# Scores between a slot's two groups of transposes, the exponential between their evictions, and a third bank for some of the transposes

## The chip, the cores and the metric

One core of a Trainium2 chip runs the whole program. TensorE (PE, with its weight loads as PEld), VectorE (DVE), ScalarE (ACT), GpSimd (POOL) and the DMA queue that SyncE (SP) issues work side by side; each takes its own instructions strictly in order, and semaphores hold an instruction back until what it reads is there and what it overwrites has been read. The metric is the time of one execution in microseconds (us), as a median of several runs.

## The reference

Three parts follow each other:

```python
q_assign = np.argmax(einsum(q_n, c_n)); k_assign = np.argmax(einsum(k_n, c_n))   # 16 clusters per head
mask = q_assign[:, :, :, None] == k_assign[:, :, None, :]
scores = np.where(mask, scale * q @ k.T, -1e9)
attn = softmax(scores); x = attn @ v                      # batch 2, 8 heads, 768 rows, head size 64
x = softplus(x @ w_in1) @ w_out1                          # 1536 tokens, 512 -> 2048 -> 512
x = (h * clip(h + 3, 0, 6) / 6) @ w_out2, h = x @ w_in2
```

Attention is confined to rows of the same cluster, and two feed-forward layers follow. The weights come as 64-bit floats.

## The kernel before, in words

Products are made of fp32r operands split into a high and a low part. The heads are worked in 8 pairs (batch by two heads); a pair has 12 slots, one for each head and block of 128 query rows, so there are 96 slots, numbered through from 0 or, where a pair is meant, from 0 to 11. A main loop runs over the slots. In slot s:

- `scores(s + 3)`: four matmuls of Q and K into a PSUM tile `s` (two of them), where two extra groups of rows carry the cluster mask; `row_max` on DVE makes `nm`, the negated row maximum; `expo` on ACT makes `pr`, the exponentials, and their row sums in `sums`.
- `flip(s, 0)` and `flip(s, 1)`: two groups of three transposes of `pr` into a PSUM bank `t`; ACT evicts a group to `pth` (high part), and DVE then makes `ptl` (low part) from `t` and `pth`. The bank is free when `ptl` is done. Pool `ps_t` has two banks, which the groups take in turn.
- `weigh`: four matmuls of `vs` (the values) with `pth` and `ptl` of three slots earlier into `pv`; after every third slot `gather` lets ACT copy `pv` to the tiles `xs`.

Around these stand `extras(s, place)`: a table written by hand (`at(slot, place, function, ...)`) that puts the rest at one of seven places of a slot, with `o` the first slot of the pair before the one that is being prepared. For the next pair: `p_sims` (cluster similarities, `psm`), `p_sims_out` (`sT`), `p_back` (transposed back, `pbk`), `p_max`, `p_equal`, `p_rank`, `p_best`, `p_first` (the first best cluster, as a one-hot matrix), `p_onehot` (transposed, `po`), `p_mask` (`mk`), and `assemble`, `assemble_mask`, which copy the pieces to Q and K by DMA. For the pair before: `total` (`rs`), `tot_flip` (`pb`), `tot_out` (`rT`), `tot_spread` (the DMAs `row` and `rsb`), `fin_*`. All PSUM tiles of this work use one bank, tag `prep` of pool `ps_p`, one after another. Weight pieces are fetched and converted at table places too (`convert_*`), and the first matmuls of the first layer (`phase_a`, tile `h`) are put into slots 88 to 96. The order within each engine is the order in which the code is written.

After the loop the two layers run; PE works through 96 steps of 12 plus 12 matmuls.

Of the kernel before, what the change touches and what calls it, by code (L numbers as in the profile page):

```python
# [8 lines left out]
F32 = mybir.dt.float32  # L9
# [13 lines left out]
def cluster_attention_then_two_mlps(  # L23
# [149 lines left out]
    def attention():  # L173
        with ExitStack() as st, ExitStack() as st_ld, ExitStack() as st_ps:
# [4 lines left out]
            pp = pool("pp", 2)  # L179
# [36 lines left out]
            cent = cb.tile([P, NPAIR * (C + D)], F32, name="cent")  # L216
            cT = cent[:, :NPAIR * C].rearrange("p (n c) -> p n c", c=C)
# [114 lines left out]
            def p_equal(n):  # L332
                d = prep[n]
                sv, mx = d["pb"], d["mx"]
                eq = sm.tile(full, F32, tag="eq", name="eq", bufs=1)
                nc.vector.tensor_tensor(eq, sv, mx.unsqueeze(2).to_broadcast(full), ALU.is_equal)
                d["eq"] = eq
# [12 lines left out]
            def p_first(n):  # L350
                d = prep[n]
                oh = sm.tile(full, BF16, tag="oh", name="oh", bufs=1)
                nc.vector.tensor_tensor(oh, d["eq"], d["mx2"].unsqueeze(2).to_broadcast(full), ALU.is_equal)
# [74 lines left out]

            def flip(t, g):
# [5 lines left out]
                pt = ps_t.tile([P, 512], F32, tag="t", name="t")  # L435
# [22 lines left out]
            def gather(h, step):  # L458
# [6 lines left out]
                if step == 0:  # L465
# [20 lines left out]
            def tot_out(n):  # L486
                rT = sm.tile([2 * NJ, P], F32, tag="rT", name="rT", bufs=1)
# [41 lines left out]
            for n in range(NP):  # L529
                o = SL * n - SL  # L530
                if n > 1:
# [19 lines left out]
                    at(o + 2, 2, p_equal, n)  # L551
                    at(o + 2, 4, p_rank, n)
                    at(o + 4, 2, p_best, n)
                    at(o + 5, 2, p_first, n)
                    at(o + 6, 3, p_onehot, n)
                    at(o + 7, 1, p_mask, n)
                    at(o + 4, 1, assemble, n, 0)
                    at(o + 7, 2, assemble_mask, n, 0)
# [26 lines left out]
                if n < NP - 1:  # L585
                    at(o + -2, 4, total, n)
                    at(o + 3, 0, tot_flip, n)
                    at(o + 3, 4, tot_out, n)
# [107 lines left out]
            c_sq = sm.tile([P, HALF], F32, tag="eq", name="c_sq", bufs=1)[:, :NPAIR * D].rearrange("p (n d) -> p n d", d=D)  # L696
# [24 lines left out]

            p_centroids(0)
# [30 lines left out]
            oh = sm.tile(full, BF16, tag="oh", name="oh", bufs=1)  # L753
            nc.vector.memset(oh, 0.0)
# [62 lines left out]
            for s in range(-3, NS + 7):  # L817
                extras(s, 0)
                if 2 <= s + 1 < NS:
                    expo(s + 1)  # L820
                extras(s, 1)
                if 2 <= s + 2 < NS:
                    row_max(s + 2)
                extras(s, 2)
                if 0 <= s < NS:
                    flip(s, 0)
# [4 lines left out]
                if 2 <= s + 3 < NS:  # L831
                    scores(s + 3)
                extras(s, 5)
                h, c = s // JH - 1, s % JH
                if 0 <= h < 4 * NP:
                    weigh(h, c)
                    if c == JH - 1:
                        for step, where in enumerate((2, 2, 4)):
# [180 lines left out]
```

## Time and profile before

| | |
|---|---|
| median of 3 runs | 782.77 us (782.29 to 786.18) |
| the profiled execution | 782.03 us |
| its span, first to last instruction | 780.2 us |
| TensorE busy in the span | 768.9 us |
| DVE, ACT, POOL busy in the span | 456.3, 416.9, 151.0 us |
| granted TensorE clock, mean | 0.999 |

The time is the whole execution; the span lies within it, and rows give times from the span's start. The attention part takes roughly the first 250 us, the layers the rest. A busy engine is not one at its peak: rows of PE overlap each other, so gaps between starts say more than busy time.

### The profile page before, as it was taken

The numbers are of one execution on the slowest core, as the hardware profiler recorded it, in microseconds if no ns is written. First come the engines' busy times: TensorE is split into PE (matmuls) and PEld (weight loads), VectorE is DVE, ScalarE is ACT, GpSimd is POOL, SyncE is SP. The second block draws the span as 40 slices with busy tenths as digits, with TensorE's granted clock in tenths as the row PEclk, the third lists the DMA queues.
The fourth block names the chain that finished last, engine by engine and source line by source line (L and its number), as shares of the span: only waits on it lengthen the run. The fifth ranks groups of instructions, "written<-read, shape, count | busy, mean of one in ns | idle before, by whom it ended". The sixth has DMA issues, their size and how long they took to land.

```text
span 780.2 us, 10575 instructions
## 1 busy us (share of the span) xinstructions
PE 768.9 (99%) x3841; PEld 642.1 (82%) x3841; DVE 456.3 (58%) x788; ACT 416.9 (53%) x830; POOL 151.0 (19%) x222
## 2 busy tenths in 40 slices
PE   7999999999999999999999999999999999999998
PEld 6788888888888788888888888888888888888886
DVE  6988888888988999721111276879752322232222
ACT  6899988988998766522122254545532222222221
POOL 3666756856434000000000000000000000000000
PEclk9999999999999999999999999999999999999999
DMA  7647667557381760000000365640000100010001
GB/s 190 186 128 178 145 158 188 136 157 172 87 249 56 267 240 0 1 1 0 1 1 27 110 207 176 210 135 0 1 1 0 55 1 0 1 55 0 1 1 54
DMA packets 39124, 69.75 MB, mean 89 GB/s; under 512 B 4480, under 2 KB 24096, under 8 KB 39072
## 3 DMA queue, kind: packets, MB, share of 16 engines
q1 hardware_dynamic: 39072, 69.08, 30.9%
q8 instruction: 30, 0.49, 0.3%
q14 instruction: 22, 0.18, 0.1%
HBM read 46.30 MB, written 3.19 MB: 63 GB/s over the span
## 4 chain that ended last, share of the span: by engine, by line
PE 88%; DVE 5%; ACT 3%; issue 1%; POOL 1%; DMA 1%; POOLq 0%; ACTq 0%; DVEq 0%; SPq 0%
PE h L169 32%; PE y L895 17%; PE y L893 16%; PE t L438 7%; PE s L408 6%; PE pv L453 6%; PE psm L308 2%; DVE ptl L443 1%; DVE nm L416 1%; ACT pth L442 1%; ACT pr L424 1%; DMA rsb<-row 0%; DMA row<-rT 0%; PE warm L245 0%; ACT xs L468 0%
## 5 line engine op out<-in xcount | busy, mean ns | idle before, releaser
L169 PE MATMUL h<-xhi,pi 128*128 128x512 f32 x768 | 238.5, 392 | 0.6 <-DVE pi L144 0.5
L169 PEld LDWEIGHTS h<-xhi,pi 128*128 128x128 f32 x768 | 143.8, 188 | 32.3 <-DVE pi L144 1.0
L874 DVE TENSOR_TENSOR glo<-g,ghi 128x512 fp32r<-128x512 f32 x96 | 66.3, 691 | 146.2 <-ACT ghi L861 117.4
L169 PE MATMUL h<-xlo,pi 128*128 128x512 f32 x384 | 149.9, 390 | 0.0
L895 PE MATMUL y<-po,ghi 128*128 128x512 f32 x384 | 118.9, 391 | 0.0
L893 PE MATMUL y<-ghi,po 128*128 128x512 f32 x384 | 118.8, 391 | 0.0
L443 DVE TENSOR_TENSOR ptl<-t,pth 128x384 fp32r<-128x384 f32 x192 | 97.8, 550 | 28.0 <-ACT pth L442 27.8
L867 DVE SCALAR_TENSOR_TENSOR g<-u,h 128x512 f32<-128x512 f32 x48 | 33.0, 688 | 127.2 <-ACT u L863 127.1
L863 ACT ACTIVATE u<-h,half 128x512 f32<-128x512 f32 x48 | 33.0, 687 | 128.3 <-PE h L169 128.0
L416 DVE TENSOR_REDUCE nm<-s 128x1 f32<-128x768 f32 x96 | 90.7, 945 | 3.7 <-PE s L408 3.7
L442 ACT ACTIVATE pth<-t 128x384 fp32r<-128x384 f32 x192 | 85.7, 487 | 11.8 <-PE t L438 11.4
L408 PE MATMUL s<-K,Q 128*128 128x256 f32 (+1 forms) x384 | 89.9, 356 | 1.7 <-ACT pr L424 1.1
L438 PE MATMUL t<-ident,pr 128*128 128x128 f32 x576 | 88.3, 280 | 1.2 <-DVE ptl L443 0.7
L424 ACT ACTIVATE pr<-s,nm 128x768 f32<-128x768 f32 x96 | 86.5, 901 | 3.5 <-DVE nm L416 3.2
L860 ACT ACTIVATE g<-h 128x512 f32<-128x512 f32 x48 | 28.5, 595 | 110.8 <-PE h L169 110.8
L169 PEld LDWEIGHTS h<-xlo,pi 128*128 128x128 f32 x384 | 72.1, 188 | 15.7
L895 PEld LDWEIGHTS y<-po,ghi 128*128 128x128 f32 x384 | 72.1, 188 | 15.6
L893 PEld LDWEIGHTS y<-ghi,po 128*128 128x128 f32 x384 | 72.0, 188 | 15.6
L438 PEld LDWEIGHTS t<-ident,pr 128*128 128x128 f32 x576 | 64.0, 140 | 20.4 <-DVE ptl L443 15.4
L408 PEld LDWEIGHTS s<-K,Q 128*128 128x128 f32 x384 | 65.8, 189 | 11.5 <-ACT pr L424 2.3
L895 PE MATMUL y<-po,glo 128*128 128x512 f32 x192 | 75.1, 391 | 0.0
L893 PE MATMUL y<-glo,po 128*128 128x512 f32 x192 | 75.0, 391 | 0.0
(123 smaller groups left out, 937.9 us busy)
## 6 DMA issues: line engine op xcount, KB each, us to landing
ri<-in_moe_w_in SPq DMA_DIRECT2D x29, 512.0 KB, 4.6
ro<-in_moe_w_out SPq DMA_DIRECT2D x29, 512.0 KB, 4.8
K<-hik SPq DMA_DIRECT2D x31, 192.0 KB, 5.3
Q<-hiq SPq DMA_DIRECT2D x15, 384.0 KB, 4.1
Q<-loq SPq DMA_DIRECT2D x16, 192.0 KB, 5.6
v<-in_v SPq DMA_DIRECT2D x8, 384.0 KB, 6.6
rsb<-row SPq DMA_DIRECT2D x16, 192.0 KB, 3.8
out<-o SPq DMA_DIRECT2D x12, 256.0 KB, 3.5
```

The costliest lines, as they stand in the source:

```text
L169: nc.tensor.matmul(hs[n][:, :TB], w[:, c, :], x[c][:, cols], start=(c == 0 and i == 0), stop=(c == NC - 1 and i == 2))
L408: nc.tensor.matmul(ps[:, n0:n1], Q[i][:, u, j * P:(j + 1) * P], K[i][:, u, n0:n1], start=(u == 0), stop=(u == 1),)
L416: nc.vector.tensor_reduce(nm, st_s[t][:, :S], AX.X, ALU.max, negate=True)
L424: nc.scalar.activation(pr, st_s.pop(t)[:, :S], AF.Exp, bias=st_p[t], accum_out=sums_of[n][:, i, j:j + 1])
L438: nc.tensor.transpose(pt[:, c * P:(c + 1) * P], pr[:, kt * P:(kt + 1) * P], ident)
L442: last_flip[:] = [nc.scalar.activation(dh, src, AF.Copy)]
L443: nc.vector.tensor_tensor(dl, src, f32(dh), ALU.subtract)
L453: nc.tensor.matmul(st_v[h][:, :HALF], vs[:, kt, i, :], st_t[h][u][:, kt, :], start=(kt == 0 and u == 0), stop=(kt == NJ - 1 and u == 1),)
L863: nc.scalar.activation(t["u"], t["h"], AF.Relu, bias=half, scale=1.0 / 6.0)
L874: nc.vector.tensor_tensor(t["glo"], t["g"], f32(t["ghi"]), ALU.subtract)
L893: nc.tensor.matmul(y[:, :TB], w[:, e, :], x, **fl)
L895: nc.tensor.matmul(y, x[:, e * P:(e + 1) * P], w.rearrange("p c e -> p (c e)"), **fl)
```

## The change

In a slot, the order of the loop changes. Before: exponential of s + 1, row_max of s + 2, both groups of transposes, scores of s + 3, weigh. Now: group 0, exponential of s + 2, scores of s + 3 and their row_max, group 1, weigh. `pr` gets a third buffer for that. In slots 4, 5, 8, 9 and 10 of pairs 1 to 6 every third group goes to the `prep` bank instead of a bank of `ps_t`: those are group 0 of slots 4 and 10 and group 1 of slots 5 and 8 (also slots 8 and 10 of pair 0). The gather of a pair's first head is one activation of all 128 partitions, with a DMA for the half that belongs to the other tile, and gathers now stand at place 0 of their slot. `p_equal`, `p_best`, `p_first`, `p_onehot`, `p_mask`, `tot_flip` and `tot_out` move to later or other places. `eq` is bf16 and holds the one-hot matrix too; `cent` borrows a load buffer, and its part `cT` is copied by POOL at the start; `oh`, `rT` and `c_sq` share buffers with other tiles.

```diff
-            pp = pool("pp", 2)
+            pp = pool("pp", 3)
...
-            cent = cb.tile([P, NPAIR * (C + D)], F32, name="cent")
-            cT = cent[:, :NPAIR * C].rearrange("p (n c) -> p n c", c=C)
+            cent = ld.tile([P, S], F32, tag="v", name="cent")[:, :NPAIR * (C + D)]
+            cT = cb.tile([P, NPAIR, C], F32, name="cT")
...
-                eq = sm.tile(full, F32, tag="eq", name="eq", bufs=1)
+                eq = sm.tile(full, BF16, tag="eq", name="eq", bufs=1)
...
-                oh = sm.tile(full, BF16, tag="oh", name="oh", bufs=1)
-                nc.vector.tensor_tensor(oh, d["eq"], d["mx2"].unsqueeze(2).to_broadcast(full), ALU.is_equal)
+                oh = d["eq"]
+                nc.vector.tensor_tensor(oh, oh, d["mx2"].unsqueeze(2).to_broadcast(full), ALU.is_equal)
...
+            def third_bank(t, g):
+                return 8 <= t < NS - SL and t % SL in (4, 5, 8, 9, 10) and (2 * t + g) % 3 == 2
+
             def flip(t, g):
...
-                pt = ps_t.tile([P, 512], F32, tag="t", name="t")
+
+                pl, tag = (ps_p, "prep") if third_bank(t, g) else (ps_t, "t")
+                pt = pl.tile([P, 512], F32, tag=tag, name="t")
...
-                if step == 0:
+                if i == 0:
+
+                    if step == 0:
+                        nc.scalar.activation(main, pv[:, :HALF], AF.Copy)
+                        nc.sync.dma_start(rest[a:a + D], main[z:z + D])
+                elif step == 0:
...
-                rT = sm.tile([2 * NJ, P], F32, tag="rT", name="rT", bufs=1)
+                rT = sm.tile([2 * NJ, P], F32, tag="sT", name="rT", bufs=1)
...
-                    at(o + 2, 2, p_equal, n)
+                    at(o + 2, 4, p_equal, n)
                     at(o + 2, 4, p_rank, n)
-                    at(o + 4, 2, p_best, n)
-                    at(o + 5, 2, p_first, n)
-                    at(o + 6, 3, p_onehot, n)
-                    at(o + 7, 1, p_mask, n)
+                    at(o + 4, 4, p_best, n)
+                    at(o + 5, 4, p_first, n)
+                    at(o + 6, 4, p_onehot, n)
+                    at(o + 6, 6, p_mask, n)
...
-                    at(o + 7, 2, assemble_mask, n, 0)
+                    at(o + 7, 1, assemble_mask, n, 0)
...
-                    at(o + 3, 0, tot_flip, n)
-                    at(o + 3, 4, tot_out, n)
+                    at(o + 3, 4, tot_flip, n)
+                    at(o + 3, 6, tot_out, n)
...
+            nc.gpsimd.tensor_copy(cT.rearrange("p n c -> p (n c)"), cent[:, :NPAIR * C])
             p_centroids(0)
...
-            oh = sm.tile(full, BF16, tag="oh", name="oh", bufs=1)
-            nc.vector.memset(oh, 0.0)
+            oh = sm.tile(full, BF16, tag="sT", name="oh", bufs=1)
+            nc.gpsimd.memset(oh, 0.0)
...
-                if 2 <= s + 1 < NS:
-                    expo(s + 1)
+                if 0 <= s < NS:
+                    flip(s, 0)
                 extras(s, 1)
                 if 2 <= s + 2 < NS:
-                    row_max(s + 2)
+                    expo(s + 2)
                 extras(s, 2)
-                if 0 <= s < NS:
-                    flip(s, 0)
+                if 2 <= s + 3 < NS:
+                    scores(s + 3)
+                    row_max(s + 3)
                 extras(s, 3)
                 if 0 <= s < NS:
                     flip(s, 1)
                 extras(s, 4)
-                if 2 <= s + 3 < NS:
-                    scores(s + 3)
                 extras(s, 5)
...
-                        for step, where in enumerate((2, 2, 4)):
+                        for step, where in enumerate((0, 0, 4)):
```

What this moves on the engines stands in the order of the built programs. First PE, slot 3 of a steady pair and the head of slot 4; `[waits ...]` names the engines whose semaphore holds a row back. Before:

```order
L483 MATMUL pb<-ident,rs 12x128 [waits DVE_49]
L438 MATMUL t<-ident,pr 128x128 [waits DVE_49]
L438 MATMUL t<-ident,pr 128x128 x2
L438 MATMUL t<-ident,pr 128x128 [waits DVE_49]
L438 MATMUL t<-ident,pr 128x128 x2
L408 MATMUL s<-K_156,Q_154 128x512 [waits DMAHW5_49,DMAHW4_49,DMAHW6_49,DMAHW3_49,Activation_49]
L408 MATMUL s<-K_156,Q_154 128x512 [waits DMAHW2_49,DMAHW7_49,DMAHW1_49,DMAHW0_49]
L408 MATMUL s<-K_156,Q_154 128x256 x2
L453 MATMUL pv<-pth,vs 128x384 [waits PE_49,Activation_49]
```

The same slot now, up to the first transposes of slot 4:

```order
L443 MATMUL t<-ident,pr 128x128 [waits DVE_49]
L443 MATMUL t<-ident,pr 128x128 x2
L408 MATMUL s<-K_157,Q_155 128x512 [waits DMAHW5_49,DMAHW4_49,DMAHW6_49,DMAHW3_49,Activation_49]
L408 MATMUL s<-K_157,Q_155 128x512 [waits DMAHW2_49,DMAHW7_49,DMAHW1_49,DMAHW0_49]
L408 MATMUL s<-K_157,Q_155 128x256 x2
L443 MATMUL t<-ident,pr 128x128 [waits DVE_49]
L443 MATMUL t<-ident,pr 128x128 x2
L493 MATMUL pb<-ident,rs 12x128 [waits DVE_49]
L458 MATMUL pv<-pth,vs 128x384 [waits PE_49,Activation_49]
L458 MATMUL pv<-ptl,vs 128x384
L458 MATMUL pv<-pth,vs 128x384
L458 MATMUL pv<-ptl,vs 128x384
L443 MATMUL t<-ident,pr 128x128 [waits Activation_49]
```

The scores now part the two groups of transposes, `pb` went behind them, and the group at the head of slot 4 waits for ACT where the others wait for DVE: it uses the bank that `pb` had.

Second, ACT in the same slot: the gathers (`xs`), the evictions (`pth`), the exponential (`pr`) and `rT`, which empties `pb`. Before:

```order
L424 ACTIVATE pr,sums<-s,nm 128x768 [waits DVE_49,Activation_49]
L466 ACTIVATE xs_1970<-pv 64x384 [waits PE_49]
L468 ACTIVATE xs_1969<-pv 64x384
L442 ACTIVATE pth<-t 128x3x128 [waits PE_49] x2
L488 ACTIVATE rT<-pb 12x128 [waits DMAHW3_49]
L424 ACTIVATE pr,sums<-s,nm 128x768 [waits DVE_49,Activation_49]
```

And now:

```order
L447 ACTIVATE pth<-t 128x3x128 [waits PE_49]
L476 ACTIVATE xs_1968<-pv 64x384 [waits PE_49]
L478 ACTIVATE xs_1967<-pv 64x384 [waits DMAHW0_49]
L447 ACTIVATE pth<-t 128x3x128 [waits PE_49,Activation_49]
L424 ACTIVATE pr,sums<-s,nm 128x768 [waits DVE_49,Activation_49]
L447 ACTIVATE pth<-t 128x3x128 [waits PE_49]
L498 ACTIVATE rT<-pb 12x128 [waits PE_49,Activation_49]
L447 ACTIVATE pth<-t 128x3x128 [waits PE_49]
```

The exponential moved from ahead of the gathers to between the evictions, so it stands between the gathers and `rT`.

Third, DVE in slots 4 and 5 of such a pair, where `p_best` (`mx<-eq`) and `p_first` (to `oh`, now to `eq`) stand. Before:

```order
L416 TENSOR_REDUCE nm<-s 128x1 [waits PE_49]
L348 TENSOR_REDUCE mx_1804<-eq 128x24 [waits Pool_49]
L443 TENSOR_TENSOR ptl<-t,pth 128x3x128 [waits Activation_49] x2
L416 TENSOR_REDUCE nm<-s 128x1 [waits DVE_49,PE_49]
L353 TENSOR_TENSOR oh<-eq,mx_1804 128x384 [waits DVE_49]
L443 TENSOR_TENSOR ptl<-t,pth 128x3x128 [waits Activation_49] x2
```

And now:

```order
L416 TENSOR_REDUCE nm<-s 128x1 [waits PE_49]
L448 TENSOR_TENSOR ptl<-t,pth 128x3x128 [waits Activation_49]
L348 TENSOR_REDUCE mx_1827<-eq 128x24 [waits Pool_49]
L448 TENSOR_TENSOR ptl<-t,pth 128x3x128 [waits Activation_49]
L416 TENSOR_REDUCE nm<-s 128x1 [waits DVE_49,PE_49]
L448 TENSOR_TENSOR ptl<-t,pth 128x3x128 [waits Activation_49]
L353 TENSOR_TENSOR eq<-eq,mx_1827 128x384 [waits DVE_49]
```

Both steps moved from ahead of the slot's `ptl` to behind its second one.

## Rows read from the trace of the kernel before

**Rows 1.** Stretches: span, busy us of PE, PEld, DVE, ACT, POOL, clock, DMA.
```profile
20.00:40.00 20.00, 18.74 (x115) 14.47 (x114) 18.90 (x32) 17.37 (x39) 12.89 (x19) 1.00 0.67 182
140.00:160.00 20.00, 19.99 (x129) 16.85 (x129) 17.93 (x31) 19.02 (x45) 17.16 (x24) 1.00 0.60 145
```

**Rows 2.** Timeline of PE: start us, length us, line, operation, tiles, shape, count.
```profile
26.19 0.94 PE L408 MATMUL s<-K,Q 128*128 128x512 f32 x4
...
135.57 0.34 PE L453 MATMUL pv<-ptl,vs 128*128 128x384 f32 x1
...
139.17 0.82 PE L438 MATMUL t<-ident,pr 128*128 128x128 f32 x6
139.74 0.95 PE L408 MATMUL s<-K,Q 128*128 128x512 f32 x4
...
141.22 0.82 PE L438 MATMUL t<-ident,pr 128*128 128x128 f32 x6
...
143.56 1.01 PE L438 MATMUL t<-ident,pr 128*128 128x128 f32 x6
...
150.72 0.33 PE L361 MATMUL po<-identb,oh 128*128 128x128 bf16 x3
...
161.52 0.82 PE L438 MATMUL t<-ident,pr 128*128 128x128 f32 x6
...
266.55 0.50 PE L169 MATMUL h<-xhi,pi 128*128 128x512 f32 x1 [0.54 <-DVE pi L144]
```

**Rows 3.** Timeline of ACT; in brackets the idle time before and its releaser.
```profile
21.00 0.67 ACT L367 ACTIVATE mk<-po,mbi,msc 128x384 fp32r<-128x384 bf16 x1 [0.36 <-PE po L361]
...
135.95 0.48 ACT L466 ACTIVATE xs<-pv 64x384 f32<-64x384 f32 x1 [1.01 <-PE pv L453]
...
139.69 0.87 ACT L442 ACTIVATE pth<-t 128x384 fp32r<-128x384 f32 x2 [0.51 <-PE t L438]
...
143.68 0.48 ACT L466 ACTIVATE xs<-pv 64x384 f32<-64x384 f32 x1
144.18 0.49 ACT L468 ACTIVATE xs<-pv 64x384 f32<-64x384 f32 x1
144.69 0.87 ACT L442 ACTIVATE pth<-t 128x384 fp32r<-128x384 f32 x2
145.45 0.25 ACT L488 ACTIVATE rT<-pb 12x128 f32<-12x128 f32 x1
145.60 0.88 ACT L424 ACTIVATE pr<-s,nm 128x768 f32<-128x768 f32 x1
...
146.48 0.89 ACT L442 ACTIVATE pth<-t 128x384 fp32r<-128x384 f32 x2
...
174.31 0.25 ACT L488 ACTIVATE rT<-pb 12x128 f32<-12x128 f32 x1
```

**Rows 4.** Groups by line, 131.84 to 160.71: busy us, mean ns, idle before, releaser.
```profile
L438 PEld LDWEIGHTS t<-ident,pr 128*128 128x128 f32 x72 | 7.9, 140 | 2.4 <-DVE ptl L443 1.8
```

**Rows 5.** Timeline of DVE, slots 51 and 52.
```profile
145.21 1.02 DVE L443 TENSOR_TENSOR ptl<-t,pth 128x384 fp32r<-128x384 f32 x2 [0.38 <-ACT pth L442]
146.15 0.95 DVE L416 TENSOR_REDUCE nm<-s 128x1 f32<-128x768 f32 x1
147.02 0.54 DVE L348 TENSOR_REDUCE mx<-eq 128x24 f32<-128x384 f32 x1
```

**Rows 6.** Timeline of the weight loads, slot 52.
```profile
146.29 0.31 PEld L438 LDWEIGHTS t<-ident,pr 128*128 128x128 f32 x3 [0.15 <-DVE ptl L443]
```

**Rows 7.** SP's queue in the timeline, and DMA issues with us to landing.
```profile
151.04 1.77 SPq L497 DMA_DIRECT2D rsb<-row  x2
...
154.40 1.22 SPq L397 DMA_DIRECT2D K<-mk  x2
...
K<-mk SPq DMA_DIRECT2D x30, 24.0 KB, 2.2
```

**Rows 8.** Timeline of POOL at the start.
```profile
4.74 0.19 POOL L290 CAST cwh<-cent 64x16 fp32r<-64x16 f32 x1
```

More of the change, by code (lines that the diff above doesn't have):

```diff
@@ L693, in attention @@
             at(99, 3, lambda: convert_rest(*pieces0[5], engine=nc.vector))
-            c_sq = sm.tile([P, HALF], F32, tag="eq", name="c_sq", bufs=1)[:, :NPAIR * D].rearrange("p (n d) -> p n d", d=D)
+            c_sq = sm.tile([P, HALF], F32, tag="mk", name="c_sq", bufs=1)[:, :NPAIR * D].rearrange("p (n d) -> p n d", d=D)
             c_ss = cb.tile([P, NPAIR], F32, name="c_ss")
```

## Prediction

> **What bounds the kernel now.** I read the stretches first. In the attention part TensorE (PE) is shown busy 19.99 of 20 us at a granted clock of 1.00, DVE 17.93 and ACT 19.02 of 20 [rows 1]. A PE that is busy all the time seems to leave nothing to gain, but matmul rows overlap (the six transposes at 139.17 are shown 0.82 long, and the scores behind them start 0.57 later [rows 2]), so what counts is the distance between starts. From slot 49 to slot 50 the transposes start 141.22 - 139.17 = 2.05 us apart [rows 2], with nothing waiting. That is PE's floor for a slot in any order of the same matmuls.
>
> Then the waits. One pair (12 slots) takes 174.31 - 145.45 = 28.86 us, read at the same instruction, rT, one pair apart [rows 3]. The eight slots 51 to 58 run from 143.56 to 161.52, 17.96 us; their floor is 8 x 2.05 plus the three one-hot transposes, whose row is 0.33 long and overlaps what follows, so 0.1 to 0.3: 16.5 to 16.7 [rows 2]. So PE waits 1.3 to 1.5 us in a pair, 1.4 from here on, nearly all of it for a transpose bank that DVE has not released: the weight loads of t lose 1.8 us of a pair to ptl [rows 4], some of which PE hides. In slots 47 to 50 nothing waits. This 1.4 us, 11 us over eight pairs, is all that a new order can win from TensorE's waits; pairs 1 to 6, the steady ones, hold 8.4 of it.
>
> The Trainium skill (Perfetto Trace Analysis, Identifying the Most-Contended Engine) says to judge TensorE by the busy share of weight loads, since matmul busy time misleads. The second half agrees with what the starts show; by the first, 16.85 of 20 us [rows 1] would leave 16%, 4.5 us a pair and 27 us over six pairs. I don't take it, because a slot without any wait shows the same gaps between loads.
>
> **The change, part by part.** Constants, from starts: PE to ACT, first transpose of a group to its eviction pth, 0.52 (139.17 to 139.69); pth to the subtraction ptl 0.52 (144.69 to 145.21) [rows 2, 3, 5]; end of ptl to the next transposes in its bank 0.06 (145.21 + 1.02 = 146.23, weight load at 146.29) [rows 5, 6]; last weigh matmul to gather 0.38 (135.57 to 135.95) [rows 2, 3]. ACT pitch: gather 0.50 and 0.51, pth 0.38 (two in 0.76), exponential with its sum 0.88 (145.60 to 146.48), rT 0.25 long [rows 3]. DVE pitch: two ptl 0.94, row_max 0.87, a step such as p_best 0.46 (its row is 0.54 long, a ptl's 0.55) [rows 5].
>
> *Ordinary slot.* PE now issues group 0, scores, group 1, weigh; ACT pth, exponential, pth; DVE ptl, row_max, ptl. Starting at 0: pth 0.52, ptl 1.04, bank free by 1.65 against 2.05 when it is wanted. Group 1 starts half a slot in, at 1.03; ACT is free for it at 0.52 + 0.38 + 0.88 = 1.78; row_max keeps DVE until 1.04 + 0.47 + 0.87 = 2.38, ptl ends at 2.93, bank free 2.99 against 3.08. No wait, though 0.1 us of slack only. So the 1.4 us can go.
>
> *Slot 3 of a pair.* Here a new wait comes. The order shows gather, gather, pth, exponential, pth, rT on ACT. gather waits for the weigh just ahead of the slot: with slot 3's first transpose at 0, the last weigh matmul starts at -0.17, gather at 0.21, pth at 0.21 + 0.50 + 0.51 = 1.22, exponential 1.60, pth 2.48, rT 2.86 to 3.11. The first transposes of slot 4 are now in the third bank, the one that rT empties, and can't start before 3.11 + 0.06 = 3.17. PE is there at 2.05 + 0.11 (tot_flip, one transpose) = 2.16. **Wait 1.0 us**, in each of pairs 1 to 6. Bounds: nothing, if slot 3 is itself late by then; 1.0 if not.
>
> *Slots 4 to 6.* p_best and p_first now stand behind the second ptl. From slot 4's start: ptl 1.04, row_max 1.51, ptl 2.38, p_best 2.85, ptl of slot 5 at 3.31, row_max 3.78, ptl 4.65, p_first 5.12, done 5.66. The one-hot transposes want it at 2 x 2.05 + 1.28 = 5.38: wait 0.3. *p_back* in slot 1 waits about 0.1 for sT, which stands behind the gathers too.
>
> *Gather for the first head* loses an activation (0.5 us) twice a pair and adds a copy on SP's queue, ahead of the mask copies. ACT is not the bound, so this is worth nothing by itself. SP: from rT to the end of the rsb issues 151.04 + 1.77 - 145.45 = 7.36 us [rows 3, 7]. rT stands 2.86 after slot 3's start, so SP is free at 10.2, after the new copy (0.6, the pitch of a mask issue, 1.22 for two [rows 7]) at 10.8; the third mask issue at 12.0, landed 2.2 later [rows 7] at 14.2. The scores that need it, in slot 9, are due after 3.16 for slot 3 with its wait, 4.10, 2.5 for slot 6 with its one-hot, 4.10 and 0.3 for the group ahead of them: 14.2. There is no margin; I put a wait of 0.1.
>
> Sum for a steady pair: 1.0 + 0.3 + 0.1 + 0.1 = 1.5 in place of 1.4. I take 0 for the six pairs, bounds +/-0.4 each, so -2.4 to +2.4. In a sentence: the waits for ptl go, and come back as one wait for rT.
>
> *Start.* The cent copy to cT runs on POOL ahead of the centroid splits that the first matmuls read. Its nearest row is a POOL cast of 0.19 us [rows 8]: 0.2 lost (bounds 0 to 0.5).
>
> *Pair 0.* DVE is busy 18.90 of 20 us there [rows 1], so at most 1.1 in 20 us, about 1.8 in the pair, can be won; I take 1.5. Against it: the mask copies for the second head go out after mk, at 21.00, and the scores that need them start at 26.19 [rows 2, 3]. From mk's start they need 0.7 for mk itself, two issues of 0.6, and 2.2 to land: 4.1. The new order puts mk behind one more exponential (about 1.4 later) and those scores ahead of their slot's second group, so they wait until about 26.5, and slot 4 starts some 0.5 later than now. Net +1.0 (0 to 1.8).
>
> *Pair 7.* rT ends slot 87 the same way, and the first matmuls of the next layer in slot 88 want that same bank: with their place 0.3 behind the slot's first transposes, they wait 0.7 (0 to 0.7). Loss 0.6.
>
> *Tail.* Expo and row_max of the last slots run one slot earlier, and nothing of scores is left there; PE waits are up to 1 us now. But what PE last waits for is weight pieces from DVE (0.54 us at 266.55 [rows 2]); behind it PE runs without a wait to the end. I take +0.6 (0 to 1.2). The bf16 eq, memset on POOL and the moved tiles change no step on the path: 0.
>
> Sum: -0.2 + 0 + 1.0 - 0.6 + 0.6 = 0.8 us gained, against the profiled execution's 782.03 (span 780.2 and 1.8 around it). The median of the runs is 0.7 above it, so the forecast is 782.77 - 0.8 = **782.0 us**; its own range, from the terms' bounds, 779 to 785.
>
> **Rivals.** *B, the waits really go.* If rT is early enough, the third bank works as meant: each of six pairs gains 1.4 - 0.3 - 0.1 = 1.0 or more, with pair 0 and the tail 1.6 - 0.8, together about 6.5: 776.3. For it: in ordinary slots no wait is left by the working above, and DVE and ACT have 10 and 5% idle. Against: the order of ACT in slot 3. It decides at rT starting 1.85 us after slot 3's start instead of 2.86. The Trainium skill (Perfetto Trace Analysis, Optimizing Tensor Performance, Matmuls) states this rule: independent groups should rotate through different PSUM banks so that eviction overlaps the next group. It leaves out that a bank borrowed from other work is free only when that work is done; no row of before shows the third bank in use.
>
> *C, slower: the masks come late.* SP's queue now has no slack before the mask copies (10.8 + 1.2 + 2.2 against 14.2). If the new copy holds SP as long as an rsb issue (0.9) or waits for its gather, or masks land 0.9 later, each of seven pairs loses about 0.9, 6 us: 788. It decides once SP is free later than 10.8 us after slot 3's start. For it: zero margin. Against: mask issues are short rows.
>
> *D, no effect at the end.* DVE's conversions set when the next layer runs free, and any gain is lost there: 782.8.
>
> **How the numbers follow.** A measurement of this kernel can tell about 0.5%, 3.9 us, from no change. Forecast 0.52, B 0.23, C 0.15, D 0.10. Forecast and D lie within 0.5% but for their edges: same 0.59; faster 0.25, slower 0.16. The range takes in the forecast, D, and the nearer halves of B and C: 776.5 to 787.
>
> **What would show it.** Right: the weight loads of t wait less for DVE and now for ACT rT, once a pair, about 1 us, in the slot after rT; rT to rT stays 28.6 to 29.1 us; one wait of po for the DVE step. Wrong: rT to rT at 27.8 or less (B); scores waiting for a DMA of mk (C); the waits in slots 51 to 58 still for ptl, since the slack of 0.1 us doesn't hold.

## The result, and the profile after

| | before | after |
|---|---|---|
| median of 8 runs each | 782.28 us | 788.86 us |
| ratio, 95% interval | | 1.0081 (1.0066 to 1.0097) |
| span of the profiled execution | 780.2 us | 787.1 us |
| span's start to start of pair 1 | 49.65 us | 49.10 us |
| pairs 1 to 6 | 171.92 us | 175.12 us |
| pair 7, slots 84 to 94 | 26.99 us | 29.40 us |
| from slot 95 to the end of the span | 531.7 us | 533.5 us |

Slower by 0.8%, outside the range. The four lower rows come from the starts of the first transposes of slots 12, 84 and 95. These are the starts of before, in PE's timeline:

```profile
49.65 0.49 PE L438 MATMUL t<-ident,pr 128*128 128x128 f32 x3
...
221.57 0.49 PE L438 MATMUL t<-ident,pr 128*128 128x128 f32 x3
...
248.56 0.49 PE L438 MATMUL t<-ident,pr 128*128 128x128 f32 x3
```

And these of after (lines have moved by five, L438 is L443 now):

```profile
49.10 0.38 PE L443 MATMUL t<-ident,pr 128*128 128x128 f32 x2
...
224.22 0.41 PE L443 MATMUL t<-ident,pr 128*128 128x128 f32 x2
...
253.62 0.49 PE L443 MATMUL t<-ident,pr 128*128 128x128 f32 x3
```

So 0.55 us were won by the start of pair 1, then 3.2 lost in the six steady pairs, 2.4 in pair 7 and 1.8 behind it: the 6.9 us of span. Lengths of slots and pairs below are such distances between starts.

What the steady pairs wait for stands in the list of waits of the weight loads (us in total, times, longest) over pairs 1 to 5. Before:

```profile
PEld t L438 <- DVE ptl L443: 8.6, 43, 0.4
```

After:

```profile
PEld t L443 <- ACT rT L498: 5.3, 5, 1.1
PEld L361 <- DVE eq L353: 3.2, 5, 0.8
PEld pbk L321 <- ACT sT L314: 0.4, 2, 0.2
```

The waits for ptl are gone altogether, and three others took their place, those the prediction named: 1.8 us a pair. The weight loads of slots 51 to 54 show the two large ones, the bracket giving the wait and what ended it:

```profile
148.14 0.31 PEld L443 LDWEIGHTS t<-ident,pr 128*128 128x128 f32 x3 [1.09 <-ACT rT L498]
...
154.25 0.17 PEld L361 LDWEIGHTS <-eq 128*128 128x128 bf16 x3 [0.62 <-DVE eq L353]
```

ACT's timeline of slot 3 is the one walked in the prediction, rT behind both gathers, both evictions and the exponential, and rT to rT is 177.21 - 147.84 = 29.37 us, against 28.86 [rows 3]:

```profile
145.19 0.48 ACT L476 ACTIVATE xs<-pv 64x384 f32<-64x384 f32 x1
145.69 0.49 ACT L478 ACTIVATE xs<-pv 64x384 f32<-64x384 f32 x1
146.21 0.49 ACT L447 ACTIVATE pth<-t 128x384 fp32r<-128x384 f32 x1
146.59 0.90 ACT L424 ACTIVATE pr<-s,nm 128x768 f32<-128x768 f32 x1
...
147.47 0.49 ACT L447 ACTIVATE pth<-t 128x384 fp32r<-128x384 f32 x1
147.84 0.25 ACT L498 ACTIVATE rT<-pb 12x128 f32<-12x128 f32 x1
...
177.21 0.25 ACT L498 ACTIVATE rT<-pb 12x128 f32<-12x128 f32 x1
```

The second wait is longer than walked because p_first is: 0.89 us instead of 0.55. DVE's timeline after the change:

```profile
152.84 0.55 DVE L448 TENSOR_TENSOR ptl<-t,pth 128x384 fp32r<-128x384 f32 x1
153.31 0.89 DVE L353 TENSOR_TENSOR eq<-eq,mx 128x384 bf16<-128x384 bf16 x1
154.12 0.55 DVE L448 TENSOR_TENSOR ptl<-t,pth 128x384 fp32r<-128x384 f32 x1
```

POOL beside it, where a cast is already running when p_first's turn comes:

```profile
153.28 0.51 POOL L377 CAST vs<-v 128x384 fp32r<-128x384 f32 x1
153.87 1.20 POOL L378 TENSOR_TENSOR vs<-v,vs 128x384 fp32r<-128x384 f32 x1
```

Before, in the same pair, DVE came first by 0.04 us, and p_first kept 0.55. Row of before, DVE's timeline:

```profile
149.27 0.55 DVE L353 TENSOR_TENSOR oh<-eq,mx 128x384 bf16<-128x384 f32 x1
```

It was POOL's step that grew there, from 1.0 to 1.38 us. POOL's timeline of before:

```profile
149.31 1.38 POOL L378 TENSOR_TENSOR vs<-v,vs 128x384 fp32r<-128x384 f32 x1
```

The trace of before held a warning, though: in pair 6 a cast had begun first and had 0.41 us to go, and p_first took 0.82 us. DVE's timeline of before:

```profile
207.00 0.82 DVE L353 TENSOR_TENSOR oh<-eq,mx 128x384 bf16<-128x384 f32 x1
```

POOL's timeline of before, beside it:

```profile
206.91 0.50 POOL L377 CAST vs<-v 128x384 fp32r<-128x384 f32 x1
```

The 20 traces (both kernels and the experiments below) hold 120 rows of p_first in pairs 1 to 6. In 91 of them a cast or a tensor_tensor of POOL is running when p_first begins and has 0.15 us or more to go; in 90 of these p_first takes what is left of it plus 0.40 to 0.43 us. (In the other one the two begin 0.02 us apart, and the cast is the one that grows.) With less left, or nothing running, p_first takes 0.55. Six rows differ: beside POOL's tensor_scalar (L271) with 1.0 us to go, it takes 0.75 to 0.77.

In pair 7 the largest wait is that of slot 93's second group. The weight loads, with the wait of h for rT that the prediction had and one for POOL's pi behind it:

```profile
235.34 0.30 PEld L169 LDWEIGHTS h<-xhi,pi 128*128 128x128 f32 x2 [0.49 <-ACT rT L498]
...
251.50 0.20 PEld L443 LDWEIGHTS t<-ident,pr 128*128 128x128 f32 x2 [1.61 <-DVE ptl L448]
...
255.90 0.19 PEld L169 LDWEIGHTS h<-xhi,pi 128*128 128x128 f32 x1 [1.17 <-POOL pi L144]
```

DVE there works on a weight piece (L117, L119), and L119, 0.68 us long elsewhere in this trace, takes 1.39 beside POOL's last step for pair 6:

```profile
248.84 0.72 DVE L117 TENSOR_SCALAR val<-val 128x512 uint32<-128x512 uint32 x1
249.60 1.39 DVE L119 SCALAR_TENSOR_TENSOR val<-ri,val 128x512 uint32<-128x512 uint32 x1
250.91 0.54 DVE L448 TENSOR_TENSOR ptl<-t,pth 128x384 fp32r<-128x384 f32 x1
```

POOL's timeline beside it:

```profile
249.36 1.07 POOL L527 TENSOR_TENSOR xlo<-xs,xhi 128x384 fp32r<-128x384 f32 x1
```

### The profile page after: what moved, and what is told of

Read it like the earlier page. It is cut to its first block, busy times and chain, and to the rows that moved or that the text cites. A ratio compares the mean times of both kernels' runs of the same rounds, so it can differ in the third digit from the quotient of the medians.

```text
span 787.1 us, 10639 instructions
## 1 busy us (share of the span) xinstructions
PE 763.2 (97%) x3841; PEld 644.0 (82%) x3841; DVE 460.8 (59%) x787; ACT 409.2 (52%) x814; POOL 150.2 (19%) x224
## 4 chain that ended last, share of the span: by engine, by line
PE 80%; DVE 8%; ACT 5%; issue 3%; POOL 2%; SPq 1%; DMA 1%; POOLq 0%; ACTq 0%; DVEq 0%
PE h L169 32%; PE y L905 17%; PE y L903 16%; PE t L443 4%; PE pv L458 4%; PE s L408 4%; DVE ptl L448 2%; DVE nm L416 2%; PE psm L308 2%; ACT pth L447 2%; ACT pr L424 1%; DVE eq L353 1%; ACT xs L478 1%; DMA K<-mk 1%; DVE val L119 1%
## 5 line engine op out<-in xcount | busy, mean ns | idle before, releaser
L448 DVE TENSOR_TENSOR ptl<-t,pth 128x384 fp32r<-128x384 f32 x192 | 105.0, 549 | 30.8 <-ACT pth L447 30.1
L447 ACT ACTIVATE pth<-t 128x384 fp32r<-128x384 f32 x192 | 94.4, 493 | 25.0 <-PE t L443 23.9
L443 PE MATMUL t<-ident,pr 128*128 128x128 f32 x576 | 95.0, 274 | 7.7 <-ACT rT L498 4.4
L870 ACT ACTIVATE g<-h 128x512 f32<-128x512 f32 x48 | 28.5, 595 | 111.1 <-PE h L169 111.1
L443 PEld LDWEIGHTS t<-ident,pr 128*128 128x128 f32 x576 | 69.8, 140 | 16.2 <-ACT rT L498 6.4
```

What stands on the lines that cost most here:

```text
L443: nc.tensor.transpose(pt[:, c * P:(c + 1) * P], pr[:, kt * P:(kt + 1) * P], ident)
L447: last_flip[:] = [nc.scalar.activation(dh, src, AF.Copy)]
L448: nc.vector.tensor_tensor(dl, src, f32(dh), ALU.subtract)
```

## The experiments

All 18 are the changed kernel with the edits shown; the time before, measured beside them, was 781.75 to 782.43. Pair 0 took from 31.7 to 33.8 us in most profiled runs, also in kernels whose code for it is the same (31.74 in e3_pair7, 33.21 in e5_pair7all): POOL waits there for a transfer, 3.3 and 4.7 us in these two, and a weight conversion waits for POOL. Medians that lie less than 1.5 us apart are therefore read through the steady pairs of the traces.

### The third bank and the wait for rT

Slot 4 without it, and no slot with it:

```diff
- t % SL in (4, 5, 8, 9, 10)
+ t % SL in (5, 8, 9, 10)          # e1_slot4
- return 8 <= t < NS - SL and ...
+ return False                     # e4_nobank
```

> Slot 4 is taken out of the list of slots with a third bank, so its first group goes back to a bank of ps_t; nothing else changes. Theory (the third bank at the head of slot 4 makes TensorE wait for rT, 1.0 us a pair, six times): the weight loads of t stop waiting for rT; some comes back as waits for ptl, since slot 3's evictions stand behind two gathers (0.2 to 0.4 a pair). Gain 3.6 to 6 us on 788.9: 783 to 785.3. Rival (ACT's order in slot 3 with its two gathers holds PE up, whichever bank is used): the wait only changes its name to ptl, at most 1.5 us gained, 787.4 or more.

> No group uses the third bank; loop order and table as after the change. Theory (in an ordinary slot of the new order a bank is free 0.1 us before it is wanted, so the third bank buys nothing there): within 1.5 us of the run without it in slot 4 alone, so 782 to 786.5, slots 5 and 7 to 10 at 2.06 to 2.15. Rival (the third bank is what takes the waits for ptl away in slots 5 and 7 to 10): each of them rises by 0.1 to 0.2, 0.6 us a pair, and the time is 3 to 6 us above that run.

Measured 788.52 and 788.22, so neither median gained more than 0.7 us, though the wait for rT went. In the first, slot 3 fell from 3.2 to 2.4 us and slot 4 rose from 2.1 to 2.4; a little more came back in slot 6, where p_first now met another POOL step and took 1.15 us, and in slot 9, where pairs 1 and 6 waited 0.9 and 0.7 us for the masks. Waits over pairs 1 to 5 in that run:

```profile
PEld L361 <- DVE eq L353: 3.0, 5, 0.7
PEld t L443 <- DVE ptl L448: 2.6, 9, 0.3
PEld s L408 <- DMA K<-mk: 0.9, 1, 0.9
```

A steady pair is 29.0 instead of 29.35. The wait for rT is real, but other limits stand about 0.35 us behind it. Of the second, the comparison in its theory held, though not the time: without any third bank pairs 1 to 5 take 29.05 us on average, without it in slot 4 alone 29.02.

### po and the masks' queue

```diff
- at(o + 6, 4, p_onehot, n)
+ at(o + 6, 6, p_onehot, n)        # e2_onehot; e7_both: and slot 4 without the bank
...
- at(o + 4, 4, tot_spread, n)
+ at(o + 7, 2, tot_spread, n)      # e8_spread: as e7_both, and this (not for pair 6)
- at(o + 9 + hf, 4, fin_scale, n, hf)
+ at(o + 10 + hf, 4, fin_scale, n, hf)
```

> The one-hot transposes po stand behind slot 6's weigh instead of ahead of it; nothing else changes. Theory (TensorE waits 0.63 us for p_first there, seven times, because p_first takes 0.89 instead of 0.55 us): by the four weigh matmuls (0.7 us) the wait is covered, slot 6 falls from 2.86 to some 2.25, gain 3.5 to 4.4 us on 788.9: 784.5 to 785.4. Rival (the masks are the limit): mk starts later, its DMAs land later, the scores of slot 9 wait for K<-mk, and the gain is under 1.5 us: 787.4 or more.

> Two earlier edits together: slot 4 without the third bank, and po behind slot 6's weigh. Theory (behind the waits for rT and for p_first stand the masks: SP issues them at 11.0 us after slot 3's start, held by rsb and the copy of the first head, so they land about 14.4, and each wait taken away ahead of that comes back as a wait of slot 9's scores): slots 3 to 8 fall by 1.2 us together, slot 9 takes 0.3 to 0.8 of it back, a steady pair is 28.9 to 29.1 and the time 786.5 to 788. Rival (the two waits were all that held a pair): 28.6 a pair and no mask wait, 784 to 785.

> As the run with both edits, and tot_spread (the two rsb issues) goes behind the mask issues on SP's queue, with fin_scale one slot later. Theory (SP's order holds the masks): masks go out as soon as mk is there, 10.0 to 10.4 after slot 3's start, slot 9 waits for nothing, a steady pair is 28.6 to 28.7, time 784 to 785.3. Rival (mk itself or the landing sets the masks' end, not SP's order): slot 9 keeps its wait, no more than 0.5 us below the run with both edits.

Measured 789.77, 788.44, 785.64. The first fell to its rival: slot 6 lost 0.5 us, but slot 7 took 0.35 of it and slot 9 waited for masks in two pairs, up to 0.8. Both edits together left 29.1 a pair, as expected of the theory, with masks issued 11.1 to 11.5 us after slot 3's start. Putting rsb behind them freed them: SP's queue in that run shows the masks ahead of rsb, issued as soon as mk was there (10.0 after slot 3's start), slot 9 waited in no steady pair, and pairs 2 to 5 took 28.8, near the 28.6 to 28.7 that its theory gave.

```profile
153.19 0.56 SPq L397 DMA_DIRECT2D Q<-mk  x1
153.80 1.21 SPq L397 DMA_DIRECT2D K<-mk  x2
...
155.69 0.60 SPq L507 DMA_DIRECT2D rsb<-row  x1
```

In the changed kernel the order is rsb, copy, masks, and SP has no pause between them:

```profile
153.36 1.81 SPq L507 DMA_DIRECT2D rsb<-row  x2
155.22 0.59 SPq L474 DMA_DIRECT2D xs<-xs  x1
155.92 0.56 SPq L397 DMA_DIRECT2D Q<-mk  x1
156.52 1.22 SPq L397 DMA_DIRECT2D K<-mk  x2
```

### The gather's copy

The two activations put back for the first head, without the copy:

```diff
-                if i == 0:
-                    if step == 0:
-                        nc.scalar.activation(main, pv[:, :HALF], AF.Copy)
-                        nc.sync.dma_start(rest[a:a + D], main[z:z + D])
-                elif step == 0:
+                if step == 0:
```

> The gather of a pair's first head is two activations again, without the copy by DMA; all else as after the change. Theory (SP's queue is the hidden cost: the copy holds it 0.6 us ahead of the masks and again in slot 9, where it waits for its gather, so loads, assembly and the last pair's rsb go out 1 to 2 us later): masks issued 0.6 to 0.7 earlier, row to rsb in pair 7 nearer to the 3.8 us of before, POOL's last work clear of DVE's conversions, pair 7 0.7 to 1.5 shorter, pair 0 about 0.5 shorter; steady pairs stay at 29.3, since rT and p_first hold them. 786.7 to 788. Rival (the copy costs nothing and spares ACT 0.5 us in two slots of a pair): the two activations lengthen slots 6 and 9, 789.5 or more.

Measured 792.5, so the rival won: slot 10 rose from 2.06 to 2.29 us with scores waiting for the exponential, a steady pair from 29.35 to 29.55, and neither pair 0 nor pair 7 became shorter. The steady pairs account for 1.1 us of the loss only; in the profiled run pair 1 started at 51.27 instead of 49.10 us. SP was freer (row to rsb in pair 7 1.7 us in place of 4.5), but in that order it wasn't what pair 7 waited for.

### Early rT

```diff
- at(o + 3, 4, tot_flip, n)
- at(o + 3, 6, tot_out, n)
+ at(o + 3, 0, tot_flip, n)        # e10_rT; e12_equal: both at (o + 3, 1)
+ at(o + 3, 1, tot_out, n)
...
- at(o + 2, 4, p_equal, n)
+ at(o + 2, 2, p_equal, n)         # e12_equal only
```

> tot_flip goes to the head of slot 3 and tot_out ahead of the exponential, so that rT is made at 1.6 us of slot 3 instead of 2.9; all else as after the change. Theory (rT's place is the first cause: it holds the third bank, and through row and rsb SP's queue and so the masks): the wait for rT at slot 4 goes, rsb and masks go out 1 us earlier, nothing comes back in slot 9 and only the wait for p_first stays; a steady pair falls from 29.35 to 28.2 to 28.6, time 782.5 to 785. Rival (as in the run without the third bank in slot 4, what is gained comes back as a wait for masks or for ptl): 28.9 a pair or more, 786 or more.

> p_equal goes back to its place of before (slot 2, ahead of row_max, so that it lets go of the prep bank about 1.1 us earlier), and tot_flip and tot_out stand behind slot 3's first group and first eviction; all else as after the change. In the run with tot_flip at the head of slot 3 TensorE waited 1.6 us there for p_equal instead of 1.0 us for rT. Theory (the prep bank is handed from pbk to pb to the third bank, and the late p_equal and late rT are the links that hold it): no wait for rT nor for p_equal, 0 to 0.4 us of ptl waits in slots 2 and 3, masks out 1.2 us earlier, a steady pair at 28.2 to 28.7, 783 to 785.5. Rival (the sum stays, the wait moves on to masks or ptl): 29 a pair or more, 786.5 or more.

The first, 789.52, showed what I had overlooked: the bank goes from pbk to pb to the third group, and p_equal, which the change made later too, still held it. Its waits over pairs 1 to 5:

```profile
PEld pb L493 <- DVE eq L336: 7.9, 5, 1.7
PEld L361 <- DVE eq L353: 1.6, 5, 0.3
```

The second, 785.43, put p_equal back: rT came at 1.64 us of slot 3, nothing waited for it, no mask was late, and two of six pairs, 1 and 6, reached 28.6 and 27.2 (pair 6 took 28.2 after the change). The others took 29.1, and what sets them apart is one wait, po's; p_first took 0.75 and 0.55 us in those two pairs:

```profile
PEld L361 <- DVE eq L353: 4.6, 5, 1.1
PEld t L443 <- DVE ptl L448: 1.5, 5, 0.4
```

In the others p_first took 1.28 to 1.32 us. DVE's timeline:

```profile
152.95 1.32 DVE L353 TENSOR_TENSOR eq<-eq,mx 128x384 bf16<-128x384 bf16 x1
```

POOL's timeline beside it:

```profile
152.85 1.00 POOL L378 TENSOR_TENSOR vs<-v,vs 128x384 fp32r<-128x384 f32 x1
153.82 1.47 POOL L271 TENSOR_SCALAR q<-q 128x384 f32<-128x384 f32 x1
```

POOL's step had begun 0.1 us before; of it 0.9 us were left, and p_first took 0.9 + 0.42.

### Pair 7 and the tail

```diff
+ LAST = NS - SL                   # from slot LAST on: expo(s + 1), row_max(s + 2),
+                                  # flip 0, flip 1, scores(s + 3), as before
...
- for step, where in enumerate((0, 0, 4)):            # e5_pair7all, not e3_pair7:
+ for step, where in enumerate((0, 0, 4) if s + 1 < LAST else (2, 2, 4)):
+ # and tot_flip, tot_out of pair 6 at (o + 3, 0) and (o + 3, 4)
...
- at(83, 0, convert_bits, *piece, 0)                  # e6_conv: eleven such lines,
+ at(83, 4, convert_bits, *piece, 0)                  # and the order kept
```

> From slot 84 on the loop takes the order of the kernel before (exponential of s+1, row_max of s+2, both groups, scores, weigh); the table of steps stays as it is after the change. Theory (in pair 7 the weight conversions on DVE stand between ptl of group 0, row_max and ptl of group 1, and the new order has no room for them): pair 7 falls from 29.4 towards 27.0 to 27.5 and the tail's 1.85 comes back: gain 3.3 to 4.2 us on 788.9: 784.7 to 785.6. Rival (the loss of pair 7 comes from elsewhere, rT ahead of h in slot 88 and POOL's subtractions ahead of the first layer): no more than 1 us gained, 787.9 or more.

> From slot 84 on everything that the change moved goes back: the loop's order, the places of the gathers, and those of tot_flip and tot_out. Theory (pair 7 and the tail lose 4.2 us against before because the new order leaves DVE's weight conversions and the early gathers no room; in the run with the order alone put back, gathers ahead of the exponential held the scores of slot 87 up for 1.6 us): pair 7 at 27.0 to 27.3, its waits those of before, end 3.5 to 4.5 us earlier than in the changed kernel's 788.9: 784.4 to 785.4. Rival (the later rT shifts POOL's work for pair 6 onto the conversions whatever the order is, or pair 7 inherits its delay from pair 6): pair 7 stays at 28.5 or more and the time at 787 or more.

> The order after the change stays in pair 7; only DVE's steps of three weight pieces (and the ACT and POOL steps tied to them) move: each stands behind the second ptl of a slot, where it stood ahead of the first one or between ptl and row_max, and one of the steps of slot 92 and 93 goes a slot later, where no row_max is left. Theory (what pair 7 lost is the place of the conversions between the two ptl): the waits of t for ptl in pair 7 fall from 4.4 to 2.5 us or less, the tail's wait for POOL's pi shrinks; gain 1.5 to 3.5 us on 788.9: 785.4 to 787.4. Rival (DVE has too much work there in any place): waits of the same sum in other slots, 788 or more.

Measured 788.47, 787.69 and 792.2. With the order put back, the way from slot 95 to the first matmul of phase B (y), 10.43 us after the change, was 8.8 in both, before's 8.78: the tail's loss is the order's (the first of the two changes nothing else). Pair 7 was not: 30.0 with the early gathers (slot 87 alone 4.5, its scores waiting for an exponential that stands behind gathers), 28.6 with all places put back. Moving the conversions alone made it 30.9, so my theory that only their places hurt fell; the new order has too little room on DVE in either of the two sets of places tried.

What kept e5_pair7all at 28.6 is mostly slot 93, 3.26 us against 2.11 (the rest is slot 84, where the two orders meet). POOL's work for pair 6 waits for rsb; rsb came late, so that work met DVE's conversions of slots 92 and 93, which took over twice as long as alone (L117 0.42, L119 0.68). SP's queue in that run:

```profile
235.34 0.32 SPq L500 DMA_DIRECT2D row<-rT  x1
...
241.12 1.13 SPq L507 DMA_DIRECT2D rsb<-row  x2
```

DVE's timeline in that run:

```profile
247.91 1.06 DVE L117 TENSOR_SCALAR val<-val 128x512 uint32<-128x512 uint32 x1
249.00 1.38 DVE L119 SCALAR_TENSOR_TENSOR val<-ri,val 128x512 uint32<-128x512 uint32 x1
```

The kernels with the old order and places in pair 7 (names as below) line up by the time from row to rsb:

| | e11 | before | e16 | e18 | e17 | e15 | e14 | e5 | e13 |
|---|---|---|---|---|---|---|---|---|---|
| row to rsb, us | 3.00 | 3.77 | 4.28 | 4.35 | 4.37 | 5.27 | 5.54 | 5.77 | 5.86 |
| L119, us | 0.87 | 0.87 | 0.87 | 0.87 | 0.87 | 1.38 | 1.39 | 1.38 | 1.38 |
| slot 93, us | 2.12 | 2.11 | 2.37 | 2.30 | 2.55 | 2.79 | 3.25 | 3.26 | 3.16 |

The landings in the traces point to what rsb, which reads row, was waiting behind. SP's last masks of pair 6 and the weight fetches behind them go out up to 3 us later in the late kernels (the masks are out 0.75 us after slot 84's start before, 3.8 in e5_pair7all). In all nine kernels rsb goes out 1.3 to 1.8 us after the landing of the last `ri` fetch (512 KB) that was issued ahead of row: at 234.60 after 232.78 us before, at 241.12 after 239.66 in e5_pair7all. For pair 7's own row and rsb, with no fetch under way, 1.4 to 2.1 us pass between the two issues. So row seems to be served behind these fetches. No run moves the fetches alone, so this is read from the traces and not tested.

### Together

```diff
  e11_all:  e10_rT, e2_onehot, e9_gather and e5_pair7all
  e13_best: e12_equal and e5_pair7all;  e14_best_nobank: without a third bank
  e15_onehot: e13_best and po at (o + 6, 6)
  e16_queue: e15_onehot, copy two slots later, four weight parts of pair 0 behind its masks
  e17_queue_nobank: e16_queue without a third bank
  e18_last: e15_onehot, copy two slots later, and
- at(max(o + -9, 4), 5, p_centroids, n)
+ at(o + -6, 5, p_centroids, n)
- at(1, 2, p_mask, 0)
+ at(1, 1, p_mask, 0)              # its masks with it
- LAST = NS - SL
+ LAST = NS - SL - 2
```

> The edits that paid, together: early rT, po behind slot 6's weigh, gather without the copy, and from slot 84 on the order and places of before; the third bank stays in all its slots. Theory (each of the four is a term of its own: rT 1.0 and p_first 0.5 in a pair, pair 7 and tail 3 to 4 us): steady pairs at 27.9 to 28.3, pair 7 at 27.0 to 27.7, time 776 to 779.5, below both kernels. Rival (a new bound, ACT in slots 3, 6 and 9 or the masks, takes the sum back): 28.6 a pair or more, 781 or more.

> The run before it plus, from slot 84 on, the order and places of before. Theory (pair 7 and tail are a term of their own, 2 to 4 us): 3 to 4 us below the run before it, 779 to 782, pair 7 at 27.4 to 27.9 (with 0.7 lost in slot 84, where the two orders meet). Rival (pair 7 stays at 28.5 as when it was put back alone, since SP's late queue comes from the steady pairs): 1.5 to 2 us below.

> The run before it without any third bank. Theory (with rT early the third bank has what it needs, and slots 4, 5, 8, 9 and 10 use it for 0.05 to 0.35 us each): 0.3 to 0.6 us a pair longer, 2 to 4 us above the run before it. Rival (ordinary slots need no third bank): within 1 us of it.

> As the run with p_equal, rT and pair 7 put back, and po behind slot 6's weigh. Theory (with rT early the last wait of a steady pair is po for p_first, 0.8 us on average, since p_first takes 1.3 us where a POOL step runs ahead of it; the masks now have slack): slot 6 falls from 3.28 to 2.5 to 2.7, slot 7 rises by 0.35 at most, pairs 2 to 5 at 28.4 to 28.8, 1.5 to 2.5 us gained: 782.5 to 783.5. Rival (masks again): slot 9 waits, less than 0.5 us gained, 784.5 or more.

> The run before it, with SP's queue rearranged: the copy of the first head's gather goes out two slots later, behind the masks, and the four parts of the first output weights in pair 0 go behind pair 0's masks. Theory (SP's queue is late from pair 0 to pair 7: pair 0 waits 2 to 3 us for its masks, pair 7's rsb lands late and POOL's last steps stretch DVE's conversions in slot 93): pair 0 at 31 to 31.8, pair 7 at 27.3 to 27.7, 2 to 4 us below the run before it, 778.5 to 781, below both kernels. Rival (the masks of pair 0 are set by mk or by landing): pair 0 stays at 32.5 or more, less than 1 us gained.

> The run before it without any third bank. Theory (where nothing else waits, the third bank is worth the 0.05 to 0.35 us of slots 4, 5 and 10): 0.2 to 0.4 us a pair longer, 1.2 to 2.5 us above the run before it. Rival (the third bank buys nothing): within 0.8 us.

> The run with po behind weigh, and four small moves: POOL's centroid splits go three slots later, behind p_values, so that a long POOL step no longer runs when p_first comes to its turn; the copy of the first head's gather goes out two slots later; pair 0's first masks are made one place earlier; the old order sets in two slots earlier, away from the weight conversions. Theory (p_first's length is set by the POOL step that runs when it begins): p_first 0.55 to 0.75 us in pairs 2 to 5 in place of 1.3, slot 6 falls to 2.3, these pairs 28.4 to 28.6; with pair 0 and pair 7 0.3 to 1 us shorter each, 780 to 782. Rival (p_first is slow by its own, on bf16 in place): 1.3 again, 783.3 or more.

Measured, in this order: 788.67, 784.98, 784.64, 784.1, 785.17, 785.55 and 779.71. The first carried p_equal's wait of 1.6 us in each pair and the cost of two more activations, so its rival came true; its pair 7 was 27.5. e13 gained 0.5 us in place of 3 to 4, since pair 7 stayed at 28.5 with row to rsb at 5.86; the tail came back to 531.7 us. Without a third bank, e14 and e17 are within 0.4 us of their partners, and their pairs 1 to 5 less than 0.1 us longer on average (pair 6 0.1 and 0.35): in these kernels, and in e4 against e1, the third bank bought next to nothing. But in all of them po still waits for p_first, and that wait hides what the bank does: without it slot 4 took 2.40 instead of 2.19 us and slot 10 0.06 more, and slot 6 gave 0.2 back. What the bank is worth once p_first is short, as in e18, no run shows. e15 brought pairs 2 to 5 from 29.1 to 29.0 only (slot 6 -0.5, slot 7 +0.35). e16 shortened slot 93 as expected, but lost more in pair 0 (slot 11 took 7.3 us): POOL's work began 1.9 us later there, behind a transfer, and a conversion step on ACT that stands ahead of an exponential waited 2.6 us for POOL.

e18 tested the last cause, together with three other small moves. POOL's long step no longer runs when p_first begins in pairs 2 to 5, and p_first was 0.55 us in all six pairs. DVE's timeline, slot 53:

```profile
150.42 0.55 DVE L353 TENSOR_TENSOR eq<-eq,mx 128x384 bf16<-128x384 bf16 x1
```

POOL's timeline beside it:

```profile
150.46 0.59 POOL L291 TENSOR_TENSOR cwl<-cT,cwh 64x16 fp32r<-64x16 f32 x1
...
151.37 0.22 POOL L291 TENSOR_TENSOR cwl<-cT,cwh 64x16 fp32r<-64x16 f32 x1
```

This time POOL's small step is the one held up, 0.59 instead of 0.22. Pairs 2 to 5 took 28.2 us. Against e15 that is 0.77 less, just what p_first lost (1.32 to 0.55); against the kernel before it is 0.7 less. Pair 1 is the exception: 29.15, with rT only 2.6 us into its slot 3 (28.44 in e15). Pair 7 took 27.2, and the time 779.71 is 0.9968 (0.9955 to 0.9982) of before's: the one version faster than both kernels, by 2.0 us against before in that comparison.

## Why the prediction was wrong

0.8 us gained were forecast and 6.9 were lost, a miss of 7.7: 3.2 in the steady pairs, 2.4 in the tail, 1.8 in pair 7, 0.25 ahead of pair 1. Two steps failed. The sum took p_first at its length without a neighbour, and it put DVE's weight conversions in pair 7 and the tail at nothing. Step by step, against the profiled execution (+ is gained):

| step | predicted | measured |
|---|---|---|
| start and pair 0 | +0.8 | +0.55 |
| six steady pairs | 0 (-2.4 to +2.4) | -3.2 |
| pair 7 | -0.6 | -2.4 |
| tail | +0.6 (0 to 1.2) | -1.8 |

- *Start, pair 0*: the sum came near by luck. Slot 0 began 0.49 us earlier, where 0.2 was to be lost (it begins between 17.1 and 18.1 us in the kernels here), and pair 0 itself won 0.06 in place of 1.0. The mask wait in slot 3 came as walked (slot 3 took 3.00 instead of 2.72), but the sum had no term for a second one, 1.16 us in slot 9.
- *Ordinary slot, slot 3 of a pair*: right. Slots 7 to 10 stand at 2.06 to 2.12 us without a wait for ptl, and the wait for rT is 1.06 where 1.0 was worked out.
- *Slots 4 to 6* is the step that failed in the steady pairs. The walk put p_first at 5.12 us after slot 4's start, and it came at 5.15; but it gave it the length of p_best's row (0.54) and so a wait of 0.3. p_first took 0.89, and the wait is 0.64. The length was right for DVE alone, but the step came 2.6 us later than before, counted from slot 3's start (8.35 against 5.71), and there a POOL step was running. e12, e15 and e18 have the same code of p_first: 1.32, 1.32 and 0.55 us, as POOL's steps beside it differ. Over six pairs this is 2.0 of the 3.2 us. The sum of waits, 1.5 forecast, is 1.8, and slots 11, 0 and 1 together grew by 0.2 (8.75 against 8.58), of which the sum had 0.1 as p_back's wait.
- *Pair 7* had the wait for rT ahead of h (0.7 forecast, 0.49) and nothing of DVE's weight conversions. The waits for ptl behind these rose from 1.8 to 4.4 us in the pair, and 1.9 of that shows in its length.
- *Tail* had the wrong sign, though the prediction itself named DVE's pieces as what PE last waits for. I counted the earlier exponentials as a gain and didn't walk DVE through slots 92 to 94: L119 came later and was 1.39 long, so POOL began the piece pi 0.96 us after slot 95's start instead of 0.63 ahead of it (254.58 against 253.62; before, 247.93 against 248.56), and PE waited 1.17 us for it.
- *Behind it PE runs without a wait to the end*: right; from the 101st matmul of y to the end it is 477.0 us in every kernel here, and the list of weight-load waits there is empty. So each us lost ahead of it is lost for good, and rival D (nothing gained arrives) does not hold.
- *Rival B* was half right. At rT 1.64 us into slot 3 the wait for it vanished, as its point of decision says, but pairs 2 to 5 fell to 28.2 only in e18, once p_equal, po and POOL's centroid steps were moved as well.
- *Rival C* named a real limit in the wrong place. The masks did not hold the steady pairs of the changed kernel (slot 9 2.07 to 2.12), because TensorE was itself late by rT and p_first; e1, e2, e4 and e7, which took one or both away, ran into the masks in one pair or more, until SP issued them ahead of rsb or rT came early.

The Trainium skill (SBUF — State Buffer, Who interferes with whom) states that a VectorE tensor_tensor whose two inputs lie in SBUF and a GpSimd step that reads SBUF exclude each other for a whole instruction, the first to start winning. In 90 of 91 rows beside a cast or tensor_tensor p_first ends 0.40 to 0.43 us after POOL's step, as this says, and all 3840 rows of ptl, with one input in PSUM, take 0.49 to 0.56 us, whatever POOL does. The six rows beside L271 do not agree: a GpSimd step that reads SBUF had 1.0 us left, and p_first was only 0.2 us longer; there the measurement decides. Weighed in the prediction, the rule would have let p_first end up to a POOL step (1.0 us, L378) later, more than the bounds of 0.4 us a pair allowed.

## What to carry to other kernels

A step of known length, moved in time, takes on the neighbours of its new place: look at what the other engines run there, above all POOL beside a DVE step that reads SBUF alone. A bank lent between two uses is as free as the slowest link of its hand-over (here pbk, p_equal, pb, rT); moving one link alone gained nothing (e10). Take one wait away and read which one stands next before pricing the gain; here the wait for rT was 1.06 us, and without it a pair was 0.35 us shorter.

## What the runs showed of the hardware

- The wait between DVE and POOL is hidden in the length of a row: p_first was 0.55, 0.89, 1.15 or 1.32 us for the same instruction, L119 0.68 to 1.39, with no idle time and no releaser in the views of before, after, e1 and e12. L117, with one input, took 0.42 us alone and 1.06 beside a POOL step in e5. Only the mean of a group, or two rows of one line side by side, gives it away.
- The same holds the other way round: POOL's subtraction of 1.0 us took 1.38 when p_first had begun 0.04 us before it, and a step of 0.22 us took 0.59.
- SP's queue issues the copy, the rsb pair and the masks one after another, at 0.6 to 0.9 us each; moving the two rsb issues behind the four mask issues took 0.3 us off each steady pair (29.1 to 28.8), with fin_scale a slot later as the only other difference.
